# Attention with projections on one core: the V loads move from SyncE's DMA queue to GpSimd's

## The chip, the cores and the metric

The kernel runs on one core of a Trainium2 chip. The metric is the device time of one execution in microseconds. TensorE (PE), VectorE (DVE), ScalarE (ACT) and GpSimd (POOL) compute; SyncE (SP) here only issues DMAs. Each engine works through its own instructions in order, and they wait for each other by semaphores. A DMA can be issued by SP or by POOL; the issuing engine waits first for what the transfer needs, and whatever stands behind the issue on that engine waits with it.

## The reference

Two problems, A and B, of the same shapes; their outputs are put side by side. For each:

```python
B, Sq, D = 16, 144, 448;  H, Sk, Dh = 16, 512, 256       # all bf16
q = (x @ wq).reshape(B, Sq, H, Dh).transpose(0, 2, 1, 3)
p = softmax(einsum("bhqd,bhkd->bhqk", q, k_cache) * Dh ** -0.5)
o = einsum("bhqk,bhkd->bhqd", p, v_cache)
out = o.transpose(0, 2, 1, 3).reshape(B, Sq, H * Dh) @ wo
```

## The kernel before, in words

One head of one batch is a *unit* `U`; there are 512 of them, A's 256 and then B's. Four units make a group `G` (128 of them), eight a super-group `SG` (64). The work on a unit is:

- **Q** (`t_q`, L325): the projection of x, 8 matmuls; DVE or ACT moves the result to `qt_sb` (L351, L355).
- **S = QK** in two parts, as the 144 query rows do not fit 128 partitions. The first 112 rows of a unit are `t_sa` (L462). The other 32 rows, the *remainder*, are done for eight units at once, `t_sb` (L367), four units side by side in one tile of 128 rows.
- **Softmax**: DVE takes the maximum (L482, L387), ACT the exponential and its sum (L493, L397), DVE the reciprocal (L503, L407), and POOL multiplies by it: the *norm* `t_norm` (L511, one a unit) and the remainder's norm `t_norm_b` (L415, one for four units).
- **P transposed**: the 112 rows on TensorE (`t_ta`, L524), moved out by DVE (L534). The remainder is transposed for eight units at once, by TensorE in the ramp and at the change from A to B, else by a DMA on SP (`t_ptb_dma`, L425). POOL then copies it, group by group, into `pt_sb` (`t_copy_ptb`, L457). So P.V of four units waits for one such copy.
- **P.V** (`t_pv`, L547 to L562): 8 matmuls, which read V from `v_sb`; ACT moves the result into `ring` (L572).
- **Output projection** (L595): pieces of it are put between the units; the result is stored by SP (L624).

K of a super-group is one transposing DMA of 2 MB into one of two slots (`t_load_k`, L306). V of a group is one DMA of 1 MB into one of five slots (`t_load_v`, L316), from 128 partitions x 4 heads, 2 KB each. Also on SP are x (L296, L297), wq (L275, L277) and wo (L285).

The order on every engine is written out ahead by one loop over slots `i` (L739 to L837). In slot `i` it adds, among other things, the DMAs that are planned for `i` (first of all), the remainder's norms, the S matmuls of the unit that `sa_slot` puts there (some 14 units ahead), the copy `t_copy_ptb` (in slots 7 and 1 of eight), the norm of the unit whose S was in slot `i - 1`, the transposes of unit `i + 2` and P.V of unit `i`. `_Sched.add` works out the semaphore waits from reads and writes, and leaves out a wait that an earlier one on the same engine already implies. A V load of group G must wait until P.V of the last unit of group G - 5 has read the slot; that is slot 4(G - 5) + 3, and `lo` in `plan_v` is the slot after it. In the steady part, with t = 8n and n = 8, 10, ..., the loads are planned at

```python
for j, at in enumerate((5, 5, 5, 8)):
    if 2 * n + 3 + j < NG:
        plan_v(t + at, 2 * n + 3 + j)
```

and in the ramp two at a time, one slot after K's (L683, L684).

Of the kernel before, what the change touches and what calls it, by code (L numbers as in the profile page):

```python
# [12 lines left out]
PE, ACT, DVE, POOL, SP = "pe", "act", "dve", "pool", "sp"  # L13
# [109 lines left out]
def bass_concat_heads__mha_block_cached__gqa_block_cached__near_ridge_kernel(  # L123
# [42 lines left out]
    NK, NV, NXG = 2, 5, 2  # L166
# [15 lines left out]
    with contextlib.ExitStack() as es:  # L182
# [28 lines left out]
        S = _Sched()  # L211
# [17 lines left out]
        def unit(U):  # L229
            pr, r = divmod(U, NU)  # L230
            b, h = divmod(r, H)
            return pr, b, h
# [77 lines left out]
        def t_load_v(G):  # L310
            pr, b, h0 = unit(4 * G)
            sl = G % NV
            src = vs[pr][b, h0:h0 + 4].rearrange("u (p c) d -> p u (c d)", p=128)

            def e(q):
                return q.dma_start(v_sb[:, sl, :, :], src).then_inc(sems["v%d" % sl], 16)  # L316
            S.add(SP, e, writes=[(("v", sl), G)], dma_sem="v%d" % sl, name="v%d" % G)

        def q_bank(U):
            if U >= 8:  # L320
# [330 lines left out]
        def plan(at, lo, dl, fn, *args):  # L651
            assert lo <= at <= dl, (fn.__name__, args, lo, at, dl)
            dma_plan.append((at, len(dma_plan), fn, args))
# [7 lines left out]

        def plan_v(at, G):
            lo = 4 * (G - NV) + 3 + 1 if G >= NV else s_min
            plan(max(at, lo), lo, 4 * G, t_load_v, G)

        def plan_pb(at, SG):
            if SG not in TB_SG:
# [3 lines left out]
        for hg in range(HG):  # L671
            plan(s_min + (0 if hg < 2 else 1), s_min, q_slot[4 * hg], t_load_wq, 0, hg)
            if hg == 1:
                plan_k(s_min, 0)
        plan_v(s_min + 2, 0)
        for n in range(1, RAMP + 2):
            at = max(sb_slot[n] - 6, sa_slot[8 * (n - NK) + 7] + 1) if n >= NK else s_min + 2
            if n == 3:
                plan_x(at, 1)
            if n == 6:  # L680
                plan_x(at, 2)
            plan_k(at, n)
            plan_v(at + 1, 2 * n - 1)  # L683
            plan_v(at + 1, 2 * n)  # L684
# [17 lines left out]
        for hg in range(HG):  # L702
            lo = q_slot[NU - H + 4 * hg + 3] + 1
# [36 lines left out]
        while True:  # L740
# [58 lines left out]
            if 0 <= u < NT:  # L799
# [9 lines left out]
                if h == H - 1:  # L809
                    g_end = pr * RP + (b + 1) * SQ  # L810
                    lo = (pr * RP + b * SQ) // 128
# [80 lines left out]
```

## Time and profile before

| what | value |
| --- | --- |
| median of three runs | 1217.22 us (1211.76 to 1221.06) |
| the profiled execution | 1215.54 us, its span 1213.8 us |
| granted TensorE clock | 0.992 |
| TensorE, matmuls | 1171.0 us busy, 96% |
| POOL | 727.9 us busy, 60%, 774 instructions |
| DMA queue of SP | 304 MB |
| V loads | 128 of 1 MB, landing 8.9 us after issue in the median |

In the rows of the profile an engine's line is followed by what it writes and reads, how often, and its time; `<-` names what ended the idle time before it. SPq is SP's own queue of issues. Times on a row of the timeline are start and length, in us from the span's start.

### The profile page before, as it was taken

To read this page: it belongs to the slowest core of one execution; us is meant where nothing else is said; L and a number is where in the kernel's file an instruction comes from. 1 tells how busy PE (TensorE), PEld (TensorE's weight loads), DVE (VectorE), ACT (ScalarE), POOL (GpSimd) and SP (SyncE) were. 2 spreads that over 40 slices of the span, in tenths; PEclk is the share of its full clock that TensorE was granted. 3 is DMA by queue.
4 is the path that set the end of the run, shared out by engine and by line. 5 is a ranking of instruction groups with operands and counts; after the bars stand their busy time and mean duration, and the time that the engine had idled before them with its cause. 6 is when DMAs were issued, how large, how long until landed. Compare 5 with 4: busy or idle time off the path is not lost.

```text
span 1213.8 us, 33200 instructions
## 1 busy us (share of the span) xinstructions
PE 1171.0 (96%) x13612; PEld 882.9 (73%) x13612; DVE 743.7 (61%) x2088; ACT 748.6 (62%) x2213; POOL 727.9 (60%) x774
## 2 busy tenths in 40 slices
PE   6898999999999999999899989999999999999989
PEld 3676777777777777777577767777777777777766
DVE  3676666656656666666566656666666566566661
ACT  2565666666656666666566656666666666566662
POOL 1675576666566666666465656666666665665661
PEclk9998999999999999999899999999999999999999
DMA  9999999999999999999999899999999999899971
GB/s 244 281 264 293 286 266 194 249 264 271 262 286 194 266 253 279 271 260 247 296 231 268 252 258 255 269 279 251 266 237 242 255 285 284 224 247 249 245 208 56
DMA packets 679577, 306.18 MB, mean 252 GB/s; under 512 B 597504, under 2 KB 610304, under 8 KB 679424
## 3 DMA queue, kind: packets, MB, share of 16 engines
q1 hardware_dynamic: 679424, 304.05, 104.6%
q8 instruction: 107, 1.75, 0.6%
q14 instruction: 46, 0.38, 0.1%
HBM read 148.90 MB, written 4.13 MB: 126 GB/s over the span
## 4 chain that ended last, share of the span: by engine, by line
PE 80%; DMA 12%; DVE 3%; POOL 2%; SPq 1%; issue 1%; ACT 1%; DVEq 0%
PE ot_ps L557 17%; PE qp_ps L338 17%; PE sa_ps L471 16%; PE op_ps L595 16%; PE sa_ps L524 7%; DMA kt_sb<-in_A_k_cache_dram 6%; DMA kt_sb<-in_B_k_cache_dram 6%; PE sb_ps L374 5%; POOL pa_sb L511 1%; DVE stat L482 1%; SPq L306 1%; POOL pb_sb L415 1%; PE sb_ps L437 1%; ACT pa_sb L493 1%; PE qp_ps L595 1%
## 5 line engine op out<-in xcount | busy, mean ns | idle before, releaser
L511 POOL TENSOR_TENSOR pa_sb<-pa_sb,stat 112x512 bf16<-112x512 bf16 x512 | 532.3, 1041 | 458.2 <-DVE stat L503 432.7
L493 ACT ACTIVATE pa_sb<-sa_ps,stat 112x512 bf16<-112x512 f32 x512 | 352.6, 689 | 405.8 <-DVE stat L482 403.6
L482 DVE TENSOR_REDUCE stat<-sa_ps 112x1 f32<-112x512 f32 x512 | 354.0, 691 | 335.3 <-PE sa_ps L471 330.7
L338 PEld LDWEIGHTS qp_ps<-xt_sb,wq_sb 128*128 128x128 bf16 x4048 | 284.1, 98 | 81.6 <-DMA wq_sb<-in_A_wq_dram 3.9
L557 PE MATMUL ot_ps<-pt_sb,v_sb 128*128 128x144 bf16 x4096 | 341.8, 226 | 0.0
L338 PE MATMUL qp_ps<-xt_sb,wq_sb 128*128 128x144 bf16 x4048 | 337.4, 227 | 4.6 <-DMA wq_sb<-in_A_wq_dram 4.2
L471 PE MATMUL sa_ps<-kt_sb,qt_sb 128*112 128x512 bf16 x1024 | 314.0, 388 | 6.0 <-DVE pt_sb L534 5.2
L595 PE MATMUL op_ps<-wo_sb,ring 128*128 128x448 bf16 x1120 | 275.1, 353 | 0.0
L557 PEld LDWEIGHTS ot_ps<-pt_sb,v_sb 128*128 128x128 bf16 x4096 | 269.5, 98 | 0.4
L524 PEld LDWEIGHTS sa_ps<-ident,pa_sb 112*128 112x128 bf16 x2048 | 159.9, 114 | 113.6 <-ACT pa_sb L493 38.3
L534 DVE COPY pt_sb<-sa_ps 128x448 bf16<-128x448 bf16 x512 | 191.4, 374 | 19.9 <-PE sa_ps L524 19.9
L572 ACT ACTIVATE ring<-ot_ps 128x288 bf16<-128x288 f32 (+8 forms) x512 | 191.0, 373 | 19.4 <-PE ot_ps L557 19.2
L524 PE MATMUL sa_ps<-ident,pa_sb 112*128 112x112 bf16 x2048 | 187.3, 213 | 6.1 <-ACT pa_sb L493 6.1
L351 DVE TENSOR_SCALAR qt_sb<-qp_ps 128x288 bf16<-128x288 f32 x252 | 115.2, 457 | 95.0 <-PE qp_ps L338 94.1
L415 POOL TENSOR_TENSOR pb_sb<-pb_sb,stat 128x512 bf16<-128x512 bf16 x128 | 133.3, 1041 | 0.0
L471 PEld LDWEIGHTS sa_ps<-kt_sb,qt_sb 128*112 128x112 bf16 x1024 | 96.8, 130 | 46.0 <-issue 28.4
L355 ACT ACTIVATE qt_sb<-qp_ps 128x288 bf16<-128x288 f32 x254 | 105.5, 415 | 33.2 <-PE qp_ps L338 31.6
L595 PEld LDWEIGHTS op_ps<-wo_sb,ring 128*128 128x128 bf16 x1120 | 96.0, 98 | 31.8 <-ACT ring L572 0.2
L493 ACT ACTIVATION_READ_ACCUMULATOR pa_sb<-sa_ps,stat 112x1 f32 x512 | 99.4, 194 | 0.0
L397 ACT ACTIVATE pb_sb<-sb_ps,stat 128x512 bf16<-128x512 f32 x128 | 88.6, 692 | 0.8
L387 DVE TENSOR_REDUCE stat<-sb_ps 128x1 f32<-128x512 f32 x128 | 87.2, 681 | 0.0
L374 PE MATMUL sb_ps<-kt_sb,qt_sb 128*32 128x512 bf16 x1024 | 69.2, 391 | 18.2 <-DMA kt_sb<-in_B_k_cache_dram 11.3
(33 smaller groups left out, 353.6 us busy)
## 6 DMA issues: line engine op xcount, KB each, us to landing
v_sb<-in_A_v_cache_dram SPq DMA_DIRECT2D x64, 1024.0 KB, 8.9
v_sb<-in_B_v_cache_dram SPq DMA_DIRECT2D x64, 1024.0 KB, 8.9
out_dram<-ost_sb SPq DMA_DIRECT2D x36, 112.0 KB, 9.7
wo_sb<-in_A_wo_dram SPq DMA_DIRECT2D x8, 448.0 KB, 9.5
wo_sb<-in_B_wo_dram SPq DMA_DIRECT2D x8, 448.0 KB, 5.2
wq_sb<-in_A_wq_dram SPq DMA_DIRECT2D x4, 768.0 KB, 6.0
wq_sb<-in_B_wq_dram SPq DMA_DIRECT2D x4, 768.0 KB, 9.7
pbt_sb<-pb_sb SPq DMA_TRANSPOSE x46, 4.9
```

The source lines that it names most:

```text
L338: ins = t.matmul(acc[:, dc * SQ:(dc + 1) * SQ], lhsT=wq_sb[:, kc, c0:c0 + 128], rhs=xt_sb[:, xsl, kc, xo:xo + SQ], start=(kc == 0 and dc = ...
L374: ins = t.matmul(sb_ps[jj // 4][32 * j:32 * j + 32, :], lhsT=qt_sb[:, U % NQT, dc, QA:SQ], rhs=kt_sb[:, dc, (U % (8 * NK)) * SK:(U % (8 * ...
L415: return g.tensor_tensor(pb_sb[:, psl, G % 2, :], pb_sb[:, psl, G % 2, :], stat[:, RINVB + sl:RINVB + sl + 1].to_broadcast([128, SK]), op= ...
L471: ins = t.matmul(sa_ps[bank][0:QA, :], lhsT=qt_sb[:, U % NQT, dc, 0:QA], rhs=kt_sb[:, dc, ko:ko + SK], start=(dc == 0), stop=(dc == 1))
L482: return v.tensor_reduce(stat[0:QA, NEG + sl:NEG + sl + 1], sa_ps[bank][0:QA, :], axis=AX.X, op=ALU.max, negate=True)
L493: return a.activation(pa_sb[0:QA, psl, :], sa_ps[bank][0:QA, :], AF.Exp, bias=stat[0:QA, NEG + sl:NEG + sl + 1], scale=1.0, accum_out=stat ...
L511: return g.tensor_tensor(pa_sb[0:QA, psl, :], pa_sb[0:QA, psl, :], stat[0:QA, RINV + sl:RINV + sl + 1].to_broadcast([QA, SK]), op=ALU.mult)
L524: ins = t.transpose(pta_ps[bank][:, c * 128:c * 128 + QA], src[:, c, :], ident[0:QA, 0:QA])
L534: return v.tensor_copy(pt_sb[:, sl, :, 0:QA], pta_ps[bank][:, 0:512].rearrange("p (c q) -> p c q", c=4)[:, :, 0:QA])
L557: ins = t.matmul(ot_ps[ob][:, dc * SQ:(dc + 1) * SQ], lhsT=v_sb[:, vsl, j, c * DH + dc * 128:c * DH + (dc + 1) * 128], rhs=pt_sb[:, sl, c, ...
L572: ins = a.activation(ring[:, 2 * h:2 * h + 2, c0:c0 + n1], src[:, :, 0:n1], AF.Copy)
L595: ins = t.matmul(acc[0:m, 0:D], lhsT=ring[:, c, col0:col0 + m], rhs=wo_sb[:, c, :], start=(c == first), stop=(c == last))
```

## The change

The V load is added to POOL instead of SP. The very first also reads the first K slot, so it is not issued before that K has landed. In the steady and late part a V load is planned no earlier than `lo + 1`, one slot later than before; with the plan above the first three of a period stay at t+5 and the fourth goes from t+8 to t+9. SP keeps K, x, the remainder's transposes, the weights and the stores.

```diff
             def e(q):
                 return q.dma_start(v_sb[:, sl, :, :], src).then_inc(sems["v%d" % sl], 16)
-            S.add(SP, e, writes=[(("v", sl), G)], dma_sem="v%d" % sl, name="v%d" % G)
+            S.add(POOL, e, reads=[(("kt", 0), 0)] if G == 0 else (), writes=[(("v", sl), G)],
+                  dma_sem="v%d" % sl, name="v%d" % G)
...
         def plan_v(at, G):
             lo = 4 * (G - NV) + 3 + 1 if G >= NV else s_min
-            plan(max(at, lo), lo, 4 * G, t_load_v, G)
+            plan(max(at, lo + 1) if G >= NV else at, lo, 4 * G, t_load_v, G)
```

Lines after L317 stand one lower in the changed kernel (L457 becomes L458).

## The prediction

> **What bounds the kernel now.** I read the page first, then the waits, the instructions of GpSimd (POOL), and last the rows of time round one group of V loads.
>
> ```profile
> PE 1171.0 (96%) x13612; PEld 882.9 (73%) x13612; DVE 743.7 (61%) x2088; ACT 748.6 (62%) x2213; POOL 727.9 (60%) x774
> ...
> DMA  9999999999999999999999899999999999899971
> ...
> q1 hardware_dynamic: 679424, 304.05, 104.6%
> ```
>
> TensorE is busy in 96% of the span, so at most 42.8 us can be won on it. The DMA engines stand at 9 tenths nearly everywhere, and all of that is on one queue. The question is therefore what the loads still cost TensorE. The waits tell it:
>
> ```profile
> PE sb_ps L374 <- DMA kt_sb<-in_B_k_cache_dram: 11.3, 5, 5.3
> ...
> PE sb_ps L374 <- DMA kt_sb<-in_A_k_cache_dram: 6.5, 4, 3.2
> ```
>
> TensorE waited 17.8 us for K and has no row at all in which it waits for V. Of the 6.5 us, all but 0.9 fall before 120 us (the waits of the window 120 to 1160 us list 0.9 for A and 11.3 for B). So 12.2 us of K waits lie in the steady part, one of them 5.3 us long, where the second problem's weights are loaded too (K issued at 582.45 us, used at 601.26).
>
> POOL is the engine that takes on work. Its groups:
>
> ```profile
> L511 POOL TENSOR_TENSOR pa_sb<-pa_sb,stat 112x512 bf16<-112x512 bf16 x512 | 532.3, 1041 | 458.2 <-DVE stat L503 432.7 <-DVE stat L407 25.4
> L415 POOL TENSOR_TENSOR pb_sb<-pb_sb,stat 128x512 bf16<-128x512 bf16 x128 | 133.3, 1041 | 0.0
> L457 POOL COPY pt_sb<-pbt_sb 128x512 bf16<-128x512 bf16 x128 | 78.2, 611 | 10.9 <-PE ot_ps L557 10.9
> ```
>
> In 16 units POOL does 16 norms (L511), 4 norms of the remainder (L415) and 4 copies (L457): 20 x 1.041 + 4 x 0.611 = 23.3 us. Sixteen units take 36.5 us (the S matmuls of the remainder, one group for every eight units, start at 164.22 and, 54 groups later, at 1149.55 in the chain of waits: 985.3 / 54 x 2). On average 13.2 us are free. But POOL works in order, and one of its results is needed soon: the copy of the transposed remainder, which P.V of the next four units reads.
>
> ```profile
> 903.67 1.04 POOL L511 TENSOR_TENSOR pa_sb<-pa_sb,stat 112x512 bf16<-112x512 bf16 x1
> 905.68 1.04 POOL L511 TENSOR_TENSOR pa_sb<-pa_sb,stat 112x512 bf16<-112x512 bf16 x1 [0.97 <-DVE stat L503]
> 906.68 1.04 POOL L415 TENSOR_TENSOR pb_sb<-pb_sb,stat 128x512 bf16<-128x512 bf16 x1
> 907.69 1.04 POOL L511 TENSOR_TENSOR pa_sb<-pa_sb,stat 112x512 bf16<-112x512 bf16 x1
> 908.68 0.61 POOL L457 COPY pt_sb<-pbt_sb 128x512 bf16<-128x512 bf16 x1
> ```
>
> ```profile
> 909.24 0.67 PE L557 MATMUL ot_ps<-pt_sb,v_sb 128*128 128x144 bf16 x8
> ...
> 911.25 0.67 PE L557 MATMUL ot_ps<-pt_sb,v_sb 128*128 128x144 bf16 x8
> ```
>
> After the norm at 903.67 POOL is idle for 0.97 us; then norm, remainder norm, norm and copy follow without a gap, and the copy ends at 909.29. The P.V that needs it starts at 911.25: **1.96 us of slack**. At 611 us the same rows stand again (idle 0.97 before 611.94, copy 614.93 to 615.54, P.V at 617.50).
>
> **The change, part by part.**
>
> *Removed from SP.* 128 issues of V, one row of the page:
>
> ```profile
> v_sb<-in_A_v_cache_dram SPq DMA_DIRECT2D x64, 1024.0 KB, 8.9
> ```
>
> Each takes 0.37 to 2.05 us of SP's queue (median 0.51). SP also waits less for freed V slots (L316: 80.8 us on the output projection, 13.7 on P.V and smaller ones), and nobody waits for SP except through K. K can now be issued when its slot is free: at 993.16 us its issue came some 9 us after the last use of the slot (the S matmuls at 984.17), behind four V, two stores, two x and a transpose of P's remainder, and TensorE waited for it. The bytes do not change and the engines are full, so K gains only in place, not in rate. I credit the 12.2 us less what is left of the long wait: that wait is 5.3 us and the slack given by the next item about 1.7 us, so 3.6 stay. **-8.6 us**; the bounds are 0 and -16.4 (the 12.2 and 4.2 in the ramp).
>
> The Trainium skill, page DMA: Bandwidth & Descriptors, section Issuing engines are not separate DMA queues, speaks against a gain here: transfers of all issuers run interleaved on the same 16 engines, and a second issuer saves only the issuing. By it the credit would be about 0; the row of queue q1, full on its own, agrees.
>
> *Added to POOL.* The 128 issues. In the built order they stand in the steady part as three in a row (planned at t+5), then norm, remainder norm, norm, copy: exactly between the rows 903.67 and 905.68 above. The fourth (planned at t+9) stands before the other copy, whose P.V is four units away (copy 913.07 to 913.68, P.V at 920.78, 7.1 us of slack). None of them has a semaphore wait except the first of all, which waits for the first K: by the time POOL comes there, it has waited for a DVE result that is younger than the P.V that frees the slot. So "one unit behind" makes the wait free, and what is left is the time C that POOL needs to issue one V load. Queued behind it are the norms and that copy, and TensorE waits for the copy.
>
> No row shows C. Lower bound: SP's shortest issue of the same transfer, 0.37 us. Upper bound: the transfer has 512 runs of 2 KB (128 partitions x 4), read and written. POOL's row of 512 elements a partition is 1.041 us, that is 2.03 ns an element; two lists of 512 at that price and SP's 0.51 for the fixed part make 2.59. I take the fixed part and one list, as the read and the write list may be made side by side: **C = 0.51 + 1.04 = 1.55 us**, between the ends and nearest to the rows of POOL itself.
>
> The Trainium skill, same page, section Anatomy of one DMA (the GpSimd path), calls descriptor generation small and says that one can emit many before the cost shows. No trace of before can show it; by it C would be the fixed 0.51 and the sum would be the first rival's.
>
> Three issues take 4.65 us. The idle 0.97 and the slack 1.96 hide 2.93, so the point from which it costs is C = 0.98. TensorE then stands **1.72 us** before P.V, once in each period with three V loads: n = 8, 10, ... 60, which is 27 periods. 27 x 1.72 = **+46.4 us**. Nothing takes it back: TensorE works in order, and the next period has the same rows.
>
> *In the ramp* two V are issued together before each of the first groups. Five early copies (52.78, 69.44, 154.87, 174.42 and 194.33 us) have only 0.3 to 1.1 us of slack; 3.1 us of issue less some 0.75 slack and 0.9 idle is 1.45, five times 7. The K waits of 4.2 us there (88.92 and 107.85 us) swallow part, as a late TensorE finds K landed, and two of the five lie ahead of them: **+1 us** net is left after I take another 2 for gaps I can't place; bounds 0 and +7. At the start the first V waits for K at 19.85 us, while POOL is idle until 26.74 (25.4 us of waiting), so three issues there (4.65) are hidden.
>
> *Sum.* 46.4 + 1 - 8.6 = +38.8 us against the profiled execution, 1215.5 us (span 1213.8 and 1.7 round it): 1254.3. The median of the runs shown, 1217.2, is 1.7 above that execution; I leave the forecast at **1254**, inside that scatter.
>
> **The rivals.**
>
> *The issue is short* (C up to 0.98). No copy is late and the K waits go: 1215.5 - 12.2 = **1203**, at the very best, with the ramp's waits too, 1199. For it: SP makes the same transfer in 0.5 us. Against: POOL's shortest work on 512 elements is 0.61 us. For C from 0.98 to 1.3 the stall eats the gain: 27 x 0.97 = 26 - 8.6 + 1 = +18 at 1.3, so 1203 to 1234.
>
> *POOL makes both lists one after the other* (C = 2.59). The stall is 7.77 - 2.93 = 4.84 us, 27 times 131: 1215.5 + 131 + 1 - 12 = **1335**. Beyond C = 3.3 (13.2 free / 4) POOL itself is the bound. For it: POOL's rows are slow per element. Against: SP needs 7.7 to 9.7 us for a K of 8192 pieces of 256 bytes, about 1 ns a piece, so lists can be cheap.
>
> *K starves beside V.* Today V stands behind K in one queue. With two queues, three V (2.65 us each by the landings 910.44, 913.10, 915.80) may run while the second K of a period is still under way. That K lands 6.2 to 7.4 us before its use (979.74 for 985.90, 1015.91 for 1023.32), so it decides from the point at which V takes over 6.2 of its 8 us from K: then 1.8 us late, 27 times, +48 and 4 less of other waits: **1259** with no POOL stall. Against: by the order POOL reaches the issue at about t+6, when K is nearly in.
>
> *The change does nothing* (V's wait was harmless and nothing gets slower): C near 1.0 and no K credit, **1216**.
>
> **How the numbers follow.** Forecast (C from 1.3 to 2.3): 0.43. Short issue: 0.28, of which 0.25 ends over 1% faster. C from 0.98 to 1.3, with the case of no effect: 0.12, of which 0.08 stays within 1%. Both lists: 0.11. K starves: 0.06. One per cent, 12 us, is about what a measurement of this kernel can tell from no change (its three runs are 9 us apart). Faster 0.25, same 0.03 + 0.08 = 0.11, slower 0.04 + 0.43 + 0.11 + 0.06 = 0.64. The range is 1201 to 1315: the low end is the short issue, the high end C = 2.3 (27 x 3.97 = 107, less 8.6); the likeliest case's own range is 1234 to 1315.
>
> **What would show it.** POOL gets 128 DMA rows of about 1.5 us, its busy share rises from 60% to about 75%, and a wait of TensorE for POOL's L458 copy appears 27 times at some 1.7 us. K's waits shrink to a few us, and a second DMA queue carries 134 MB. It is wrong if those POOL rows are under 1 us or not there, if P.V never waits for the copy, or if TensorE's new waits are on K or V.

## The result and the profile after

The changed kernel's median is **1261.56 us** (1247.79 to 1266.22, four runs) against 1216.67 us before: **1.0346 times as long, interval 1.0301 to 1.0391**, some 42 us by the ratio. The profiled execution took 1247.79 us, its span is 1245.9 us: 32.1 us longer than the span before. It is the shortest of the four, so the trace shows the smaller part of the loss.

The page of the changed kernel: busy time of the engines, then the DMA queues (packets, MB, share of 16 engines).

```profile
PE 1176.4 (94%) x13612; PEld 885.8 (71%) x13612; DVE 744.6 (60%) x2088; ACT 748.6 (60%) x2213; POOL 821.1 (66%) x902
...
q1 hardware_dynamic: 611840, 169.83, 72.7%
q0 software_dynamic: 34816, 134.23, 31.5%
```

TensorE does the same work, 5 us longer, at a granted clock of 0.985 (0.992 before); the rest of the loss is waiting. 134.23 MB went to a second queue. A V load there is 34816 / 128 = 272 packets, nearly all of 4 KB; K stays on q1 in pieces of 256 bytes. POOL is 93 us busier.

The groups of POOL in the changed kernel (times, busy us, mean ns, idle before):

```profile
L316 POOL DMA_DIRECT2D v_sb<-in_A_v_cache_dram x64 | 49.3, 774 | 18.4 <-DMA kt_sb<-in_A_k_cache_dram 18.4
L316 POOL DMA_DIRECT2D v_sb<-in_B_v_cache_dram x64 | 49.0, 769 | 0.0
```

An issue costs POOL **0.77 us**; the prediction had taken 1.55. Now the waits (us in total, times, longest):

```profile
PE sb_ps L375 <- DMA kt_sb<-in_B_k_cache_dram: 16.5, 6, 5.0
PE sb_ps L375 <- DMA kt_sb<-in_A_k_cache_dram: 14.5, 5, 7.2
...
PE sb_ps L438 <- POOL pb_sb L416: 8.9, 8, 1.7
...
PE ot_ps L558 <- DMA v_sb<-in_A_v_cache_dram: 6.8, 1, 6.8
...
PE ot_ps L558 <- POOL pt_sb L458: 0.3, 1, 0.3
```

The row of the norm before:

```profile
PE sb_ps L437 <- POOL pb_sb L415: 1.0, 1, 1.0
```

TensorE waits for K 31.0 us, where it was 17.8; once 6.8 us for V, which it never did; for POOL's norm of the remainder 8.9 us, where it was 1.0; and for POOL's copy 0.3 us in all, where 46.4 had been forecast. With the 5.4 us of longer work, these waits (13.2, 6.8, 7.9 and 0.3 more) make 33.6 us, about the 32.1 by which the span grew. The timeline of POOL shows why the copy is not late:

```profile
930.91 2.27 POOL L316 DMA_DIRECT2D v_sb<-in_B_v_cache_dram  x3
933.20 1.05 POOL L512 TENSOR_TENSOR pa_sb<-pa_sb,stat 112x512 bf16<-112x512 bf16 x1
934.20 1.05 POOL L416 TENSOR_TENSOR pb_sb<-pb_sb,stat 128x512 bf16<-128x512 bf16 x1
935.20 1.04 POOL L512 TENSOR_TENSOR pa_sb<-pa_sb,stat 112x512 bf16<-112x512 bf16 x1
936.18 0.60 POOL L458 COPY pt_sb<-pbt_sb 128x512 bf16<-128x512 bf16 x1
```

The three issues stand where they were expected, ahead of norm, remainder norm, norm and copy. They take 2.27 us, less than the 2.93 us that idle time and slack hide.

The waits for the norm are another matter. They come in the ramp, where TensorE transposes the remainder itself and needs its norm at once. Two issues stand right ahead of that norm on POOL:

```profile
64.75 1.53 POOL L316 DMA_DIRECT2D v_sb<-in_A_v_cache_dram  x2
66.30 1.05 POOL L416 TENSOR_TENSOR pb_sb<-pb_sb,stat 128x512 bf16<-128x512 bf16 x1
...
67.40 0.40 PE L438 MATMUL sb_ps<-ident,pb_sb 128*128 128x128 bf16 x4 [1.59 <-POOL pb_sb L416]
```

This wait comes five times between 67 and 136 us, with 1.59 to 1.66 us each.

**Where the time went** is read from the start of the remainder's S matmuls (L375), one group for every eight units, each of which needs a new K; I count these and their K from 0. The second group starts at 40.89 us before and at 55.11 after (+14.2); group 8 is 18.3 us late (the waits for the norm come on top here, and two K waits of the ramp are gone); from there the delay grows in steps, above all at groups 16, 18, 46, 47, 58 and 59, to 32.1 at the end. Between the steps it stays constant within 0.1 us for many groups at a time, or shrinks by at most 1.5. These rows of the timeline (after) show the start:

```profile
19.65 40.68 SPq L306 DMA_TRANSPOSE kt_sb<-in_A_k_cache_dram  x2
...
19.79 2.42 POOL L316 DMA_DIRECT2D v_sb<-in_A_v_cache_dram  x3 [18.41 <-DMA kt_sb<-in_A_k_cache_dram]
...
42.12 1.12 PE L558 MATMUL ot_ps<-pt_sb,v_sb 128*128 128x144 bf16 x8 [6.77 <-DMA v_sb<-in_A_v_cache_dram]
...
55.11 1.47 PE L375 MATMUL sb_ps<-kt_sb,qt_sb 128*32 128x512 bf16 x12 [7.20 <-DMA kt_sb<-in_A_k_cache_dram]
```

The second K and the first three V are issued within 2 us, on two queues. The V land at 41.99, 44.76 and 47.55 us, the K at 55.06: 35.4 us after its issue, where it took 16.7 before. The rows before the change, with one V ahead of that K in the same queue and two behind it:

```profile
20.06 0.59 SPq L316 DMA_DIRECT2D v_sb<-in_A_v_cache_dram  x1
20.69 14.45 SPq L306 DMA_TRANSPOSE kt_sb<-in_A_k_cache_dram  x1
35.18 1.13 SPq L316 DMA_DIRECT2D v_sb<-in_A_v_cache_dram  x2
...
40.89 1.05 PE L374 MATMUL sb_ps<-kt_sb,qt_sb 128*32 128x512 bf16 x16
```

Then one of the later steps, at group 46:

```profile
866.82 14.17 SPq L306 DMA_TRANSPOSE kt_sb<-in_B_k_cache_dram  x1
...
885.49 0.83 PE L375 MATMUL sb_ps<-kt_sb,qt_sb 128*32 128x512 bf16 x12 [3.46 <-DMA kt_sb<-in_B_k_cache_dram]
```

The fourth V of the period was issued on POOL at 862.19 and landed at 874.80; the K issued at 866.82 ran beside it and landed at 885.45, after 18.6 us. What both got in a part of that time (DMA view of the changed kernel, 867.5 to 874 us; packets, MB, share):

```profile
q1 hardware_dynamic: 1114, 0.28, 75.6%
q0 software_dynamic: 266, 1.02, 55.9%
```

In 6.5 us SP's queue moved 0.28 MB, 43 GB/s, and V 157 GB/s. The window mixes two things. From 871 to 872.5 us the packets alternate, 135 of V (0.55 MB) and 137 of K (0.04 MB). From 867 to 869 us there are 189 of K and 24 of V, and both together get only 70 GB/s. From group 10 to the end a period's first K, which has an even number, takes 15.0 us from issue to landing in the median against 13.0 before, and it had 0.9 us of slack; the second one takes 11.9 against 11.5, with 6.9 us of slack before (both from the issue and landing of each K).

### The profile page after: what moved, and what is told of

The parts are those of the page before. It is cut to its first block, busy times and chain, and to the rows that moved or that the text cites. A ratio compares the mean times of both kernels' runs of the same rounds, so it can differ in the third digit from the quotient of the medians.

```text
span 1245.9 us, 33200 instructions
## 1 busy us (share of the span) xinstructions
PE 1176.4 (94%) x13612; PEld 885.8 (71%) x13612; DVE 744.6 (60%) x2088; ACT 748.6 (60%) x2213; POOL 821.1 (66%) x902
## 3 DMA queue, kind: packets, MB, share of 16 engines
q0 software_dynamic: 34816, 134.23, 31.5%
## 4 chain that ended last, share of the span: by engine, by line
PE 74%; DMA 17%; POOL 3%; DVE 2%; SPq 1%; issue 1%; ACT 1%; DVEq 0%
PE ot_ps L558 16%; PE qp_ps L339 15%; PE sa_ps L472 15%; PE op_ps L596 15%; DMA kt_sb<-in_B_k_cache_dram 9%; DMA kt_sb<-in_A_k_cache_dram 8%; PE sa_ps L525 6%; PE sb_ps L375 5%; POOL pa_sb L512 2%; DVE stat L483 1%; POOL pb_sb L416 1%; SPq L306 1%; POOL v_sb L316 1%; PE sb_ps L438 1%; ACT pa_sb L494 1%
## 5 line engine op out<-in xcount | busy, mean ns | idle before, releaser
L375 PE MATMUL sb_ps<-kt_sb,qt_sb 128*32 128x512 bf16 x1024 | 69.6, 393 | 31.3 <-DMA kt_sb<-in_B_k_cache_dram 16.5
```

Of the source, the lines that this page charges most:

```text
L375: ins = t.matmul(sb_ps[jj // 4][32 * j:32 * j + 32, :], lhsT=qt_sb[:, U % NQT, dc, QA:SQ], rhs=kt_sb[:, dc, (U % (8 * NK)) * SK:(U % (8 * ...
```

## The experiments

**1. The two queues by themselves.** Does the loss come from sharing the DMA engines, and what share does each queue get? Nothing is computed here: only K and V are moved, in stages, each begun when the one before has landed. It was executed once. The code shown is the sixth stage.

```python
# stages: 4 K on SP | 8 V on SP | 8 V on POOL | 8 V on ACT | K,V,V x4, all on SP
#   | 4 K on SP beside 8 V on POOL | 4 K on SP beside 8 V on ACT
#   | 8 V on SP beside 8 V on POOL | 4 K on SP beside 2 V on POOL
for i in range(NK):
    load_k(i)
for i in range(NV):
    load_v("p", i)
barrier()
```

> This kernel computes nothing of the reference: it only moves data, in nine stages, each begun when the one before has landed: 4 K alone (transposing, 2 MB each), 8 V alone on SP, 8 V alone on POOL, 8 V alone on ACT's queue, 4 K and 8 V in turn on SP, 4 K on SP beside 8 V on POOL, 4 K on SP beside 8 V on ACT, 8 V on SP beside 8 V on POOL, 4 K on SP beside 2 V on POOL. From the landings before, a K takes about 9 us and a V 2.65, so K and V in one queue are 36 + 21 = about 57 us. Theory 1, the engines are shared without loss: K on SP beside V on POOL is 57 us too, V ends first and each K that runs beside V takes much longer. Theory 2, the mixture itself is slow (at the start of the changed kernel 35.4 us for what took 24.9): beside POOL it is 70 to 80 us. Rival, POOL's queue is slow by itself: V alone on POOL takes over 28 us where SP takes 23, and K beside V on ACT is 57.

Measured, from a stage's first issue to its last landing:

| stage | us |
| --- | --- |
| 4 K alone | 34.7 |
| 8 V on SP, on POOL, on ACT, each alone | 25.0, 25.6, 24.8 |
| K, V, V four times in SP's queue | 59.3 |
| 4 K on SP beside 8 V on POOL | 60.5 (the first K after 36.7) |
| 4 K on SP beside 8 V on ACT | 57.7 (the first K after 28.2) |
| 8 V on SP beside 8 V on POOL | 46.7 |
| 4 K on SP beside 2 V on POOL | 48.8 (the first K after 24.6) |

POOL's queue is not slow: alone it moves V as fast as SP's. Eight V and four K need 60.5 us, the sum of both alone (34.7 + 25.6 = 60.3), so a second queue adds no bandwidth; what changes is whose turn it is. The DMA view of this kernel while V ran, 180 to 188 us:

```profile
q0 software_dynamic: 698, 2.71, 89.7%
q1 hardware_dynamic: 699, 0.18, 10.8%
```

**The two queues take turns packet by packet, 698 to 699.** A turn of V is 4 KB, one of K 256 bytes: V gets 339 GB/s, K 22 (alone V gets 349 and K 247, the second and the first row below). From ACT, V goes in 2 KB packets, and K gets 44 GB/s (0.53 MB in 12 us). Short mixes also lose in sum: with two V the stage takes 48.8 us, where one after the other they would take 34.7 + 2 x 2.7 = 40. The windows view (start:end, length, POOL busy, clock, DMA share, GB/s):

```profile
1.00:35.00 34.00, 0.00 (x0) 1.00 1.15 247
...
62.00:86.00 24.00, 5.23 (x8) 1.00 0.96 349
...
200.00:208.00 8.00, 0.00 (x0) 1.00 1.22 176
...
346.00:355.00 9.00, 0.00 (x0) 1.00 1.19 153
```

Where a V load nears its end beside K (200 to 208, 346 to 355 us), the rate falls to 176 and 153 GB/s, below that of either alone. The kernel is in this regime at its start: from 23 to 40 us it moves 192 GB/s, before the change 292. Why it falls isn't shown. The DMA view has a hint, from 204 to 207 us:

```profile
q1 hardware_dynamic: 324, 0.08, 126.1%
q0 software_dynamic: 19, 0.07, 6.1%
```

V is down to some 6 packets in a us, and still K gets no more than 108 packets in a us, 28 GB/s. If these last V packets lie on one of the 16 DMA engines and K goes forward on all 16 in step, 16 x 6 = 96 would be expected. The view doesn't name the engine of a packet, so this is an estimate and not shown.

**2. The start undone:** the changed kernel with the first three V back on SP. **3. The start alone:** the kernel before with only these three on POOL.

```diff
+            sp = G < 3            # in 3: sp = G >= 3, V planned as before, and the first V still reads the first K slot
...
-            S.add(POOL, e, reads=[(("kt", 0), 0)] if G == 0 else (), writes=[(("v", sl), G)],
+            S.add(SP if sp else POOL, e, reads=(), writes=[(("v", sl), G)],
```

> The changed kernel, but the first three V loads are back on SP. Theory: the second K, which landed at 55.1 us in place of 37.3 beside three V, is 14 to 19 us of the 45 us lost; this kernel takes 1242 to 1247. If instead the loss comes from POOL's time for its issues (128 times 0.77 us), the start was hidden there and this kernel stays at 1261.

> The kernel before, but the first three V loads go through POOL, after the first K has landed. Theory: 14 to 19 us slower than before, 1231 to 1236, with the second K landing near 55 us. If only the steady part mattered: 1217.

In both, the V of each queue have semaphores of their own. Run 2: 1247.56 us, 1.0247 times before (1.0204 to 1.0290), that is 1% less than the full change. Run 3: 1228.81 us, 1.0108 (1.0070 to 1.0147). Both put the start at 12 to 13 us (8 to 18 by the interval of run 3), below the 14 to 19 expected. In run 3 the second K lands 36.7 us after its issue and the same wait stands in the timeline, with no V on POOL after it:

```profile
56.91 1.90 PE L378 MATMUL sb_ps<-kt_sb,qt_sb 128*32 128x512 bf16 x16 [7.21 <-DMA kt_sb<-in_A_k_cache_dram]
```

So the start is a part of its own, and the smaller one.

**4. The fourth V back on SP as well:** run 2, and the fourth V of each steady period on SP; the other three stay on POOL.

```diff
-            sp = G < 3
+            sp = G < 3 or (G >= 22 and G % 4 == 2)
```

> The changed kernel, but the first three V loads and the fourth of every period in the steady part are on SP; three of four stay on POOL. Theory: what is lost in the steady part comes from the fourth V, which POOL issues just before or beside the K that is due next; in one queue the two don't overlap, and this kernel takes 1217 to 1226. Rival, every V on POOL costs alike: about three quarters of the steady loss stay, some 1237 to 1240.

1215.87 us (ten runs), **0.9992 times before (0.9974 to 1.0011)**. Against run 2 only the fourth V differs: 1.0247 - 0.9992 is 31 us. The waits of run 2 and then of run 4 after 120 us:

```profile
PE sb_ps L378 <- DMA kt_sb<-in_B_k_cache_dram: 20.3, 7, 4.8
...
PE sb_ps L378 <- DMA kt_sb<-in_A_k_cache_dram: 10.7, 5, 5.0
...
PE ot_ps L561 <- POOL pt_sb L461: 4.4, 3, 2.4
```

```profile
PE sb_ps L378 <- DMA kt_sb<-in_B_k_cache_dram: 8.9, 3, 6.1
...
PE sb_ps L378 <- DMA kt_sb<-in_A_k_cache_dram: 1.1, 2, 0.9
```

31.0 us of waiting for K become 10.0. The 4.4 us of run 2 for POOL's copy become 0.3: there POOL itself had waited 8.8 us for the remainder's transpose, a small DMA on SP that came late as well. The three V that POOL issues in a row, which the forecast and its rival had argued about, cost nothing that can be measured in the steady part: neither through POOL's time nor through the odd K beside them. The median even K takes 12.7 us again. In the ramp POOL's time still costs: TensorE waits 9.9 us for the norm of the remainder in run 4 as in run 2, and run 4 is 2.3 us late at group 8 of its profile; by the end that is made up.

**5. The stall on POOL, made on purpose.** Was the step about POOL's order wrong, or only its price? The kernel before gets, once in each of the 27 periods, work for POOL at the place of the three issues: seven multiplications of a scratch tile, no DMA moved.

```diff
+            for j in range(7):
+                S.add(POOL, e, reads=[("scr", 0)], writes=[("dm", (n, j))], name="dm%d" % n)
...
+            if 8 * RAMP <= i < NT - 26 and i % 16 == 5:
+                t_dummy(i)
```

> The kernel before, with V on SP as before, and seven multiplications of a spare 128x304 tile added on POOL where the changed kernel has its three V issues (27 places, planned at t+5). They take about 7 x 0.67 = 4.7 us, what the prediction gave to three V issues. If its step is right that 2.93 us are hidden and TensorE stands for the rest, this is 27 x 1.77 = 48 us slower, 1265, with TensorE waiting for POOL's copy of the remainder. If the slack was misread, 1217.

1279.56 us, 1.0499 times before (1.0461 to 1.0536): 61 us. Its timeline (start, length), and its waits:

```profile
912.08 5.32 POOL L313 TENSOR_TENSOR dm_sb<-dm_sb,stat 128x304 bf16<-128x304 bf16 x7
...
920.33 0.61 POOL L470 COPY pt_sb<-pbt_sb 128x512 bf16<-128x512 bf16 x1
```

```profile
PE ot_ps L570 <- POOL pt_sb L470: 56.7, 27, 2.8
```

By the prediction's arithmetic 27 x (5.32 - 2.93) = 64.5 us; 56.7 us of waits in 27 places came, 2.1 us each. So the place and the count were right, and the cover is 5.32 - 2.1 = 3.2 us in place of 2.93; only the price of an issue was far off. That the time agrees even better, 61 us, is in part luck: the K waits shrink from 17.8 to 7.5 us, and TensorE's matmuls take 17.5 us longer (1188.5 us, at a granted clock of 0.983).

**6. The fourth V later, on POOL:** run 2 with the fourth V planned at t+15 instead of t+8 (which `lo + 1` makes t+9), behind the next even K in time.

```diff
-            for j, at in enumerate((5, 5, 5, 8)):
+            for j, at in enumerate((5, 5, 5, 15)):
```

> All V but the first three stay on POOL; only the fourth of each period is issued later, planned at t+15 in place of t+9, when the K that is due next should be in and the one after it is not yet issued. Theory 1, V takes the engines' turns from the K that runs beside it: nearly all of the 32 us that the fourth V cost are gone, 1216 to 1226. Rival, any V on POOL costs some 1 us wherever it stands: 1245.

1226.24 us (median of nine runs), 1.0053 (1.0021 to 1.0086). On the same queue, with only the time of issue changed, 24 of the 31 us are gone. Its profiled execution (1230.18 us) waits 21.6 us for K after 120 us, 10.1 of them at the change from A to B, where one K takes 29.2 us; the kernel before waits 5.3 us there, for a K that takes 18.7. What this K shares the engines with wasn't taken apart.

**7. The same place in SP's queue:** the kernel before, all V on SP, with the fourth V planned behind the next even K. **8. Run 7 with x moved as well.**

```diff
-            for j, at in enumerate((5, 5, 5, 8)):
+            for j, at in enumerate((5, 5, 5, 13.5)):
...
-                plan_x(t - 4, XG)      # run 8 only
+                plan_x(t - 2, XG)
```

> The kernel before, all V on SP; only the fourth V of each period is planned behind the next K in the one queue (13.5 in place of 8). If the lesson is that K's place in the queue decides and V has time, the K waits of the steady part (12.2 us) shrink by 6 to 10 us: 1207 to 1211. If K's lateness comes from K's own issue (its slot, its transposes), 1217.

> As the run before, and x is planned behind that K too (t-2 in place of t-4). Its two transposes are 0.9 us of the engines and 1.5 us of SP's queue, one period in two: 0 to 4 us less than the run before, 1205 to 1211.

Run 7: **1207.55 us, 0.9907 (0.9878 to 0.9935)**, shorter than both kernels. Run 8: 1207.27 us, 0.9903 (0.9874 to 0.9932), so x adds nothing that can be told. The waits of run 7 after 120 us:

```profile
PE sb_ps L374 <- DMA kt_sb<-in_B_k_cache_dram: 4.1, 2, 3.7
PE sb_ps L374 <- DMA kt_sb<-in_A_k_cache_dram: 1.2, 2, 0.7
```

The K waits of the steady part fall from 12.2 to 5.3 us, and the median slack of the even K grows from 0.9 to 3.2 us: one number in the plan gives some 7 us of the 11, without a second queue. In the profiled executions TensorE's matmuls also take 4.3 us less (1166.7 us for 1171.0, at a granted clock of 0.997 for 0.992); whether the plan brings that about isn't shown.

## Why the prediction was right in its number and wrong in its reason

The forecast of 1254 lies 8 us below the measured median, and slower was right. **That is a coincidence: the term that carried it is not there.** What came instead is, in kind, the rival *K starves beside V*, which was given 0.06.

- *Added to POOL, the price C.* This is the step that failed. C was put at 1.55 us from POOL's row per element, on the notion that POOL goes through a list of 512 runs at that speed. It is 0.77, under the threshold of 0.98, so 46.4 us became 0.3. The lower bound of 0.37 held it. The Trainium skill, page DMA: Bandwidth & Descriptors, section Anatomy of one DMA, which calls descriptor generation small, was nearer: by it the prediction would have taken the fixed 0.51. The threshold itself was sound: with the 3.2 us of cover of run 5 it is 1.07.
- *Removed from SP, the K credit.* -8.6 us had the wrong sign: 12.2 us of K waits in the steady part became 22.3. The step said that K gains "only in place, not in rate". It counted what leaves the queue in front of K and not what then runs beside K. While V stood in SP's queue, K had the engines for itself once its turn came (290 GB/s from 30 to 36 us of the kernel before, in packets of 256 bytes alone); beside a V on the second queue it doesn't (22 GB/s in run 1).
- *The start.* That three issues there are hidden was true of POOL's time and false of their transfers. POOL reaches them at 19.79 us, while the second K is issued; before, only one V went ahead of that K and two behind it. That cost 12 to 13 us, for which the sum had nothing.
- *In the ramp.* The +1 us (0 to +7) was near: the delay grows by 4.1 us from the second group to group 8. But the wait is not at the copies, where five times 1.45 us was put with C = 1.55. It is at the norm of the remainder, behind two issues that take 1.53 us, five times 1.6 us, with nothing to hide them. The ramp's K waits of 1.0 and 3.2 us (groups 4 and 5) did go, as forecast.
- *The rival K starves.* Its mechanism is the measured one, its place is not. It looked at the odd K beside three V, with 6.2 to 7.4 us of slack, and priced that at 48 us. Run 4 shows that this pair costs nothing. The loss is at the even K beside the single fourth V, 31 us, where the slack is 0.9 us, and at the start. The median of the slack by kind of K, to be had from the trace of before, would have pointed there.
- *Short issue* (1203) was right in C and wrong in taking the K waits to vanish with it.
- *Both lists* (1335) had C at 2.59, more than three times what it is; *no effect* (1216) is ruled out by the interval of the ratio.
- *The tell-tales.* 134 MB on a second queue came. POOL rows of 1.5 us, 75% busy and 27 waits for the copy did not (0.77 us, 66%, one wait), and "new waits on K or V" had been named as what would make it wrong.

The sum of the parts in medians: 12 us (start) and 31 us (fourth V) against 42 measured, with run 4, which keeps the ramp and three V of four on POOL, 1 us below before. In the profiled execution the split is 14 us for the start, 4 for the ramp and 14 after group 8; in that of run 2 the part after group 8 costs 30. I take that for scatter: whether an even K is late turns on a slack of 0.9 us, and the four runs of the change are 18 us apart.

## What to carry to other kernels

In these runs a second DMA queue added no bandwidth to full DMA engines (60.5 us for 60.3 in run 1); it gave up the order of a single queue, and with it the priority of the load that is due next. Before a load is moved, list for every load that can then run beside it its slack and its packet size, and look at the shortest slack, not the typical one. When the urgent load is a few us late, put the load that can wait behind it in the same queue. On the engine that issues, look at what stands right behind the issue: three of them (2.27 us) cost nothing ahead of work with 2.93 us of cover, and two (1.53 us) cost TensorE 1.6 us ahead of the norm that it waited for.

## What the runs showed of the hardware

- Queues of different issuers alternate packet by packet on the DMA engines, so the share of bytes goes with packet size: 339 to 22 GB/s for 4 KB against 256 bytes. The Trainium skill, page DMA: Bandwidth & Descriptors, section Queues, rings and completion order, says that each engine goes round the queues by whole packets; the 698 to 699 agree with it.
- The same load goes out in packets of 4 KB from POOL (issue 0.75 to 0.77 us of its time) and of 2 KB from ACT.
- A transposing load beside a copy that is nearly done can pull the sum down to 153 GB/s, where each alone gets 247 and 349. The Trainium skill, same page, section Issuing engines are not separate DMA queues, has transfers of all issuers interleave; the long stage agrees (60.5 us for 60.3), the short one is 9 us worse than one after the other.
